# Attention preparation in a fused attention and feed-forward kernel: one lead for every pair of heads, loads listed by attention position, VectorE work in single pieces

## The chip, the cores and the metric

The kernel runs on one core of one Trainium2 chip. The metric is device time in microseconds (us) of one execution. The kernel before took 451.32 us in the median of 20 runs (449.64 to 452.49).

## What is computed

Attention with 8 batches, 8 heads, a sequence of 1152 and a head dimension of 64, whose queries are averaged in neighbouring twos (so 576 queries per head), is followed by a feed-forward block on 4608 tokens of width 512. Cut to what matters:

```python
q_pool = q.reshape(B, H, S // 2, 2, D).mean(axis=3)
scores = (1.0 / np.sqrt(D)) * np.matmul(q_pool, k.transpose(0, 1, 3, 2))
attn = np.exp(scores - scores.max(-1, keepdims=True)); attn = attn / attn.sum(-1, keepdims=True)
x = np.matmul(attn, v).transpose(0, 2, 1, 3).reshape(B * 576, 512)   # 4608 x 512
a = x @ w1                     # 4608 x 1024
b = x @ w2                     # 4608 x 1024
out = (a * b @ w3) @ w_out     # 4608 x 512
```

The kernel multiplies `w3` and `w_out` once (its T), so that the last line is one product per token tile.

## The kernel before

Two heads form a pair; there are 32 pairs, numbered P. The scores of all pairs, laid end to end, are cut into chunks of 512 columns per head. An iteration `it` of the main loop (162 of them) issues two chunks. A pair is 5184 such columns, or 5.06 iterations, and the attention position `at` is `it * 1024 / 5184`, in pairs.

One iteration emits, in this order, onto the engines:

- TensorE: the score matmuls of two chunks (`scores`, L187), which read `kT[P]` and `qT[P]`, the transposed keys and queries. ScalarE: one exponential per chunk (`expo`, L193) from the PSUM tile `psc` (two buffers) into the ring `er`.
- Preparation of later pairs, if it is due (see below).
- TensorE: the products of finished exponentials with `vt` (`attend`, L206) into the PSUM tile `po`, of which there is one buffer. When a pair is complete, `normalize` (L216, L218) has VectorE write `xn`, which frees `po`, and SyncE's queue transposes `xn` into `xT` by two DMAs.
- TensorE: filler. `fill(due)` pulls matmuls from generators until a count of modelled TensorE time, `busy`, reaches `due`, which grows by `PACE0` or `PACE1` in each iteration. The fillers are `gen_T` (transposes of `w3`, L250, and products with `w_out`, L265), from iterations `T_AT` on, and `gen_ffn` (L278, L291, L301), one unit per 512 tokens, from three iterations after the attention of its tokens is done. Filler and preparation share the two PSUM buffers of tag `ff`. What is left of the filler after the loop, and the last two units, run in a tail.

Each engine carries out its own instructions in the order in which they are emitted. The order is written by hand (`manual_schedule`); waits between engines come from the tiles and their buffer counts.

Preparation of pair P starts from three loads, `load(P)`: keys into `kst` (4 buffers, L90), queries into `qst` (3 buffers for two pairs each, L83), values into `vst` (4 buffers, L97). All loads, those of the weights too, go out from GpSimd's queue in the order of emission, and cast from 4-byte to 2-byte numbers. A DMA from this queue uses one of eight semaphores in turn, so it is issued only when the eighth DMA before it has landed; a load into a reused buffer also waits until VectorE has read the old contents.

- Pairs 0 to 7 (`NPE`): `prep_stage` emits three VectorE operations at once, the sum of neighbouring queries (`pool_q`, L119), a reordering copy of the keys into `kc` (L148) and the copy of the values into `vt` (L128), 0.8 pairs ahead. `prep_pe`, 0.5 pairs ahead, finishes the filler's open PSUM group (`fill(0, settle=True)`) and then emits 18 TensorE transposes (L158, L163) and three copies out of PSUM (L164, L168, L169), ahead of the iteration's `attend`. Those transposes are not added to `busy`. For pair 0 ScalarE makes the large copy (L166).
- Pairs from 8 on: `prep_dma` emits the three VectorE operations (L135, L119, L128) and two transposing DMAs on SyncE's queue (L136 into `kT`, L138 into `qT`) in one iteration. Its lead is 1.0 pair for pair 8, 1.5 for pair 9 and 1.6 from pair 10 on:

```python
lead = 0.5 if prepped < NPE else min(1.6, 0.5 + 0.5 * (prepped - NPE + 1))
```

For even P from 8 on, one `pool_q` sums the queries of P and P+1 together.

Of the kernel before, what the change touches and what calls it, by code (L numbers as in the profile page):

```python
# [8 lines left out]
FP16 = mybir.dt.float16  # L9
# [6 lines left out]
NJ = 9  # L16
# [7 lines left out]
def kernel(  # L24
# [11 lines left out]
    nc = tc.nc  # L36
    B, H, S, D = q.shape
# [5 lines left out]
    NP = B * H // 2  # L43
    SCL = 16.0
    NPE = 8
    T_AT = (8, 14)

    T_MM, T_TR, T_SC, T_AV = 0.216, 0.06, 0.63, 0.061
    PACE0, PACE1 = 2.2, 2.19
    SCALE = 0.5 * float(D) ** -0.5  # L50

# [2 lines left out]
    ab = ctx.enter_context(tc.tile_pool(name="ab", bufs=4))  # L54
    ffp = ctx.enter_context(tc.tile_pool(name="ffp", bufs=2))
    psum = ctx.enter_context(
        tc.tile_pool(name="psum", bufs=1, space=bass.MemoryType.PSUM))

    xT = const.tile([128, NC, NT], FP16)
    w1sb = const.tile([128, NC, dff], FP16)  # L60
    w2sb = const.tile([128, NC, dff], FP16)
# [6 lines left out]
    ident = const.tile([128, 128], FP16)  # L68
# [7 lines left out]
    kst, vst, qst, kT, qT, qps = {}, {}, {}, {}, {}, {}  # L76

    def load_q(P):
        if P % 2 == 0:
            qst[P // 2] = stage.tile([128, 2, 18, D], FP16, tag="qst", bufs=3, name="qst")  # L80
        b, h0 = P // 4, 2 * (P % 4)
        o = 64 * (P % 2)
        nc.gpsimd.dma_start(  # L83
            out=qst[P // 2][o:o + 64].rearrange("p u t d -> p u (t d)"),
            in_=q[b, h0:h0 + 2].rearrange("u (p t) d -> p u (t d)", t=18))

    def load_k(P):
        b, h0 = P // 4, 2 * (P % 4)
        kst[P] = stage.tile([128, 2, NJ, D], FP16, tag="kst", name="kst")
        nc.gpsimd.dma_start(  # L90
            out=kst[P].rearrange("p u j d -> p u (j d)"),
            in_=k[b, h0:h0 + 2].rearrange("u (p j) d -> p u (j d)", j=NJ))

    def load_v(P):
        b, h0 = P // 4, 2 * (P % 4)
        vst[P] = stage.tile([128, 2, NJ, D], FP16, tag="vst", name="vst")
        nc.gpsimd.dma_start(  # L97
            out=vst[P].rearrange("p u j d -> p u (j d)"),
            in_=v[b, h0:h0 + 2].rearrange("u (p j) d -> p u (j d)", j=NJ))

    def load(P):
        if P < NP:
            load_k(P)
            load_q(P)
            load_v(P)

    def pool_q(P):

        pp, o = P // 2, 64 * (P % 2)
        if P % 2 == 0:  # L110
            qps[pp] = ab.tile([128, NJ, 2, D], FP16, tag="qp", bufs=2, name="qp")
        if P < NPE:
            r = slice(o, o + 64)
        elif P % 2 == 0:
            r = slice(0, 128)
        else:
            return
        src = qst[pp][r].rearrange("p u (c two) d -> p u c two d", two=2)
        nc.vector.tensor_tensor(  # L119
            out=qps[pp][r].rearrange("p c u d -> p u c d"),  # L120
            in0=src[:, :, :, 0, :], in1=src[:, :, :, 1, :], op=ALU.add)

    def new_kq(P):
        kT[P] = ab.tile([128, NJ, 128], FP16, tag="kT", bufs=3, name="kT")
        qT[P] = ab.tile([128, NJ, 64], FP16, tag="qT", bufs=3, name="qT")

    def copy_v(P):
        nc.vector.tensor_copy(out=vts[P % 4][:, :, :, 0:D], in_=vst.pop(P))  # L128

    def prep_dma(P):  # L130

        pp, o = P // 2, 64 * (P % 2)
        new_kq(P)
        kc = ab.tile([128, NJ, 2, D], FP16, tag="kc", bufs=2, name="kc")
        nc.vector.tensor_copy(out=kc.rearrange("p j u d -> p u j d"), in_=kst.pop(P))  # L135
        nc.sync.dma_start_transpose(out=kT[P], in_=kc.rearrange("p j u d -> p (j u d)"))  # L136
        pool_q(P)
        nc.sync.dma_start_transpose(  # L138
            out=qT[P], in_=qps[pp][o:o + 64].rearrange("p c u d -> p (c u d)"))
        copy_v(P)  # L140

    kcs = {}

    def prep_stage(P):

        pool_q(P)
        kcs[P] = ab.tile([128, NJ, 2, D], FP16, tag="kc", bufs=2, name="kc")
        nc.vector.tensor_copy(out=kcs[P].rearrange("p j u d -> p u j d"), in_=kst.pop(P))  # L148
        copy_v(P)

    def prep_pe(P):
        pp, o = P // 2, 64 * (P % 2)
        new_kq(P)
        kc = kcs.pop(P)
        t2 = psum.tile([128, 1024], FP16, tag="ff", bufs=2, name="t2")
        t1 = psum.tile([128, 1024], FP16, tag="ff", bufs=2, name="t1")
        for c in range(NJ):
            nc.tensor.transpose(t2[:, 128 + 64 * c:192 + 64 * c],  # L158
                                qps[pp][o:o + 64, c].rearrange("p u d -> p (u d)"),
                                ident[o:o + 64, o:o + 64])  # L160
        for j in (8, 0, 1, 2, 3, 4, 5, 6, 7):
            dst = t1[:, 128 * j:128 * j + 128] if j < 8 else t2[:, 0:128]
            nc.tensor.transpose(dst, kc[:, j].rearrange("p u d -> p (u d)"), ident)  # L163
        nc.vector.tensor_copy(out=qT[P].rearrange("p c f -> p (c f)"), in_=t2[:, 128:704])  # L164
        if P == 0:
            nc.scalar.copy(out=kT[P][:, 0:8].rearrange("p j f -> p (j f)"), in_=t1)  # L166
        else:
            nc.vector.tensor_copy(out=kT[P][:, 0:8].rearrange("p j f -> p (j f)"), in_=t1)  # L168
        nc.vector.tensor_copy(out=kT[P][:, 8], in_=t2[:, 0:128])  # L169


    psc = {}
# [60 lines left out]
    def load_w3(i):  # L233
        t = ffp.tile([128, 4, dff], FP16, tag="g", name="w3h")
        nc.gpsimd.dma_start(
            out=t, in_=moe_w3.rearrange("(c p) f -> p c f", p=128)[:, 4 * i:4 * i + 4])
        w3h.append(t)

    def load_w(dst, src):
        nc.gpsimd.dma_start(out=dst, in_=src.rearrange("(c p) f -> p c f", p=128))  # L240
# [31 lines left out]
    def gen_ffn(t, tail):  # L272
# [25 lines left out]
        for i in range(4):  # L298
# [13 lines left out]
            for s in range(2):  # L312
# [13 lines left out]
        out=ident, in_=ident, compare_op=ALU.not_equal, fill=1.0,  # L326
        base=0, channel_multiplier=1, pattern=[[-1, 128]])
    load_v(0)
    load(1)
    load(2)  # L330
    load_w3(0)
    load_w(wosb, moe_w_out)
    load(3)
    load_w3(1)
    waiting = [lambda: load(4), lambda: load_w(w1sb, moe_w1), lambda: load_w(w2sb, moe_w2),
               lambda: load(5), lambda: load(6)]
    loaded, staged, prepped = 7, 1, 1
    prep_stage(0)
    prep_pe(0)

    n_units = NT // 512
    filler = []
    next_unit = 0
    busy = due = 0.0
# [4 lines left out]
    def fill(until, settle=False):  # L349

        nonlocal busy, whole
        while filler and (not whole if settle else busy < until):
            try:
                cost, whole = next(filler[0])
                busy += cost
            except StopIteration:
                filler.pop(0)

    for it in range(NIT):
        if it in T_AT:  # L360
            filler.append(gen_T(T_AT.index(it)))

        while next_unit < n_units:
            last_b = (512 * (next_unit + 1) - 1) // SQ
            if (last_b + 1) * 4 * PAIR + 3 * 2 * CH > it * 2 * CH:
                break
            filler.append(gen_ffn(next_unit, False))
            next_unit += 1
        scores(2 * it)
        expo(2 * it)  # L370
        scores(2 * it + 1)
        expo(2 * it + 1)
        busy += T_SC
        due = (due if filler else busy - T_SC) + (PACE0 if it < 20 else PACE1)
        at = it * 2 * CH / PAIR
        if staged < NPE and at >= staged - 0.8:
            prep_stage(staged)
            staged += 1
            if waiting:
                waiting.pop(0)()  # L380
                if waiting:
                    waiting.pop(0)()
            else:
                load(loaded)
                loaded += 1
        lead = 0.5 if prepped < NPE else min(1.6, 0.5 + 0.5 * (prepped - NPE + 1))
        if prepped < NP and at >= prepped - lead:
            if prepped < NPE:
                fill(0, settle=True)
                prep_pe(prepped)  # L390
            else:
                prep_dma(prepped)
                load(loaded)
                loaded += 1
            prepped += 1
        ready = [b for b in blocks[nb:nb + 40]
                 if b[0] * SQ + min(128 * b[1] + 128, SQ) <= 2 * it * CH]

        last = [n for n, (J, i) in enumerate(ready) if J % NJ == NJ - 1 and i == 4]
        if last:  # L400
            ready = ready[:last[0] + 1]
        busy += T_AV * len(ready)
        for J, i in ready:
            attend(J, i)
        if last:
            normalize(ready[-1][0] // NJ)
        nb += len(ready)
        fill(due)
    for J, i in blocks[nb:]:
        attend(J, i)  # L410
    normalize(NP - 1)
# [37 lines left out]
```

The softmax here doesn't subtract the row's maximum and nothing guards it: scores larger than these inputs give would overflow.

## Time and profile before

| | us |
|---|---|
| median of 20 runs | 451.32 |
| the profiled execution, its own time | 451.45 |
| its span, first to last instruction | 449.7 |
| TensorE matmuls busy | 419.6 |
| ScalarE busy | 329.9 |
| VectorE busy | 198.3 |

1.75 us of the profiled execution lie outside its span. Matmuls are pipelined and their ends are modelled, so a TensorE that shows busy is not TensorE at its peak; what counts is where it is idle. In a line of the timeline the columns are start, duration, engine, line, operation, tiles written and read, shape where it is kept, the number of instructions merged, and in brackets the engine's idle time before it with what ended it. In the table of waits the columns are the waiting line, what it waited for, the sum in us, the number of times and the longest. PE is TensorE's matmul row, PEld its weight loads, ACT ScalarE, DVE VectorE, POOL GpSimd, SPq the queue of SyncE.

### The profile page before, as it was taken

To read this page: it belongs to the slowest core of one execution; us is meant where nothing else is said; L and a number is where in the kernel's file an instruction comes from. 1 tells how busy PE (TensorE), PEld (TensorE's weight loads), DVE (VectorE), ACT (ScalarE), POOL (GpSimd) and SP (SyncE) were. 2 spreads that over 40 slices of the span, in tenths; PEclk is the share of its full clock that TensorE was granted. 3 is DMA by queue.
4 is the path that set the end of the run, shared out by engine and by line. 5 is a ranking of instruction groups with operands and counts; after the bars stand their busy time and mean duration, and the time that the engine had idled before them with its cause. 6 is when DMAs were issued, how large, how long until landed. Compare 5 with 4: busy or idle time off the path is not lost.

```text
span 449.7 us, 12036 instructions
## 1 busy us (share of the span) xinstructions
PE 419.6 (93%) x5168; PEld 223.1 (50%) x5168; DVE 198.3 (44%) x347; ACT 329.9 (73%) x350; POOL 69.7 (15%) x107
## 2 busy tenths in 40 slices
PE   1889899999599999999999999999999999989996
PEld 1555464554255555555555555545555555544442
DVE  2245453565145534554345444544455344433130
ACT  2877777778388888888878888888888888823332
POOL 7312131113011111111111111111100000000000
PEclk9999999999699999999999999999999999999999
DMA  8999999658999989998899999969892461121304
GB/s 129 209 182 207 210 188 190 97 89 121 118 200 156 146 145 166 172 138 131 137 189 134 128 147 203 134 112 171 163 153 64 88 103 25 15 67 41 88 7 93
DMA packets 94468, 59.11 MB, mean 131 GB/s; under 512 B 66256, under 2 KB 83664, under 8 KB 94416
## 3 DMA queue, kind: packets, MB, share of 16 engines
q0 software_dynamic: 25168, 33.56, 48.6%
q1 hardware_dynamic: 69248, 24.79, 35.5%
q8 instruction: 40, 0.66, 0.6%
q14 instruction: 12, 0.10, 0.1%
HBM read 67.11 MB, written 9.44 MB: 170 GB/s over the span
## 4 chain that ended last, share of the span: by engine, by line
PE 83%; DMA 5%; ACT 4%; DVE 4%; issue 3%; SPq 1%; POOL 0%; ACTq 0%; DVEq 0%; POOLq 0%
PE po L206 21%; PE psc L187 20%; PE pb L291 13%; PE pa L278 13%; PE pp L301 12%; ACT er L193 3%; PE pT L265 3%; DMA qT<-qp 3%; DMA kst<-in_k_dram 1%; PE t L163 1%; DVE xn L218 1%; DVE kT L168 1%; PE w3t L250 1%; DMA out_dram<-osb 1%; DVE T L269 0%
## 5 line engine op out<-in xcount | busy, mean ns | idle before, releaser
L193 ACT ACTIVATE er<-psc 128x1024 f16<-128x1024 f32 x324 | 313.5, 1022 | 72.1 <-PE psc L187 69.2
L187 PE MATMUL psc<-qT,kT 64*128 64x512 f16 (+7 forms) x1152 | 109.4, 291 | 11.3 <-DMA qT<-qp 5.5
L206 PE MATMUL po<-vt,er 128*128 128x65 f16 x2880 | 116.7, 194 | 0.3 <-DVE xn L218 0.2
L206 PEld LDWEIGHTS <-er 128*128 128x128 f16 x2880 | 97.5, 98 | 35.5 <-issue 32.0
L187 PEld LDWEIGHTS <-kT 64*128 64x128 f16 x1152 | 44.2, 95 | 95.8 <-issue 84.2
L291 PE MATMUL pb<-xT,w2sb 128*128 128x512 f16 x288 | 79.7, 379 | 2.4 <-DVE osb L310 1.3
L278 PE MATMUL pa<-xT,w1sb 128*128 128x512 f16 x288 | 79.1, 379 | 1.2 <-DVE asb L287 0.7
L296 DVE TENSOR_TENSOR gT<-pb,asb 128x512 f16<-128x512 f32 x72 | 49.6, 689 | 64.1 <-PE pb L291 63.6
L301 PE MATMUL pp<-T,gT 128*128 128x512 f16 x288 | 71.0, 382 | 0.0
L287 DVE COPY asb<-pa 128x512 f32<-128x512 f32 x56 | 38.6, 689 | 47.0 <-PE pa L278 47.0
L90 POOL DMA_DIRECT2D kst<-in_k_dram x32 | 22.9, 715 | 221.1 <-DVE kc L135 174.7
L310 DVE TENSOR_SCALAR osb<-pp 128x512 f32<-128x512 f32 x28 | 19.3, 690 | 53.4 <-PE pp L301 51.0
L301 PEld LDWEIGHTS <-gT 128*128 128x128 f16 x288 | 25.5, 98 | 24.4 <-issue 0.6
L278 PEld LDWEIGHTS <-w1sb 128*128 128x128 f16 x288 | 25.8, 97 | 23.8 <-issue 0.7
L291 PEld LDWEIGHTS <-w2sb 128*128 128x128 f16 x288 | 25.4, 97 | 23.6 <-issue 1.6
L285 ACT COPY asb<-pa 128x512 f32<-128x512 f32 x16 | 9.4, 586 | 24.5 <-PE pa L278 24.5
L218 DVE TENSOR_TENSOR xn<-po,rz 128x640 f16<-128x640 f32 x32 | 26.4, 825 | 1.3 <-DVE rz L216 0.2
L97 POOL DMA_DIRECT2D vst<-in_v_dram x32 | 23.2, 725 | 16.4 <-DMA w3h<-in_moe_w_dram 5.6
L216 DVE RECIPROCAL rz<-po 128x10 f32<-128x10 f32 x32 | 7.1, 221 | 38.1 <-PE po L206 38.0
L83 POOL DMA_DIRECT2D qst<-in_q_dram x32 | 19.6, 612 | 8.9 <-DMA w2sb<-in_moe_w_dram 4.2
L119 DVE TENSOR_TENSOR qp<-qst 128x1152 f16<-128x1152 f16 (+1 forms) x20 | 15.0, 751 | 6.4 <-DMA qst<-in_q_dram 6.3
L265 PE MATMUL pT<-wosb,w3T 128*128 128x512 f16 x64 | 16.5, 379 | 1.2 <-DVE w3T L252 1.2
(29 smaller groups left out, 96.5 us busy)
## 6 DMA issues: line engine op xcount, KB each, us to landing
qst<-in_q_dram POOLq DMA_DIRECT2D x32, 288.0 KB, 6.9
kst<-in_k_dram POOLq DMA_DIRECT2D x32, 288.0 KB, 5.3
vst<-in_v_dram POOLq DMA_DIRECT2D x32, 288.0 KB, 9.1
out_dram<-osb SPq DMA_DIRECT2D x72, 128.0 KB, 3.1
w3h<-in_moe_w_dram POOLq DMA_DIRECT2D x2, 1024.0 KB, 20.5
wosb<-in_moe_w_out_dram POOLq DMA_DIRECT2D x1, 1024.0 KB, 19.3
xT<-xn SPq DMA_TRANSPOSE x64, 3.5
w1sb<-in_moe_w_dram POOLq DMA_DIRECT2D x1, 1024.0 KB, 21.4
```

The lines of the kernel that those rows point to most:

```text
L90: nc.gpsimd.dma_start(out=kst[P].rearrange("p u j d -> p u (j d)"), in_=k[b, h0:h0 + 2].rearrange("u (p j) d -> p u (j d)", j=NJ))
L97: nc.gpsimd.dma_start(out=vst[P].rearrange("p u j d -> p u (j d)"), in_=v[b, h0:h0 + 2].rearrange("u (p j) d -> p u (j d)", j=NJ))
L187: nc.tensor.matmul(t[:, u, o:o + ln], kT[P][s, j, :], qv[s, f0:f0 + ln], start=True, stop=True)
L193: nc.scalar.activation(out=er[:, :, r:r + CH], in_=psc.pop(c), func=AF.Exp, bias=0.0, scale=SCALE)
L206: nc.tensor.matmul(po[P][:, u, VW * i:VW * i + D + 1], er[:, u, r:r + 128], vts[P % 4][:, u, j, 0:D + 1], start=(j == 0 and i == 0), stop= ...
L218: nc.vector.tensor_tensor(out=xn.rearrange("p i u d -> p u i d"), in0=acc[:, :, :, 0:D], in1=rz.to_broadcast([128, 2, 5, D]), op=ALU.mult)
L265: nc.tensor.matmul(pt, w3T[:, c, a, :], wosb[:, a, :], start=(a == 0), stop=(a == NF - 1))
L278: nc.tensor.matmul(pa, w1sb[:, mc, ft * 128:ft * 128 + 128], xT[:, mc, t0:t0 + 512], start=(mc == 0), stop=(mc == NC - 1))
L287: nc.vector.tensor_copy(out=asb, in_=pa)
L291: nc.tensor.matmul(pb, w2sb[:, mc, ft * 128:ft * 128 + 128], xT[:, mc, t0:t0 + 512], start=(mc == 0), stop=(mc == NC - 1))
L296: nc.vector.tensor_mul(out=gT[:, ft, :], in0=pb, in1=asb)
L301: nc.tensor.matmul(pp, gT[:, ft, 128 * i:128 * i + 128], T16[:, ft, :], start=(ft == 0), stop=(ft == NF - 1))
```

## The change

- `prep_dma` is split into `dma_k` and `dma_q`, `prep_stage` into `pool_q`, `copy_k` and `copy_v`. Each becomes an entry of a list `side`, and one entry is taken per iteration, after the filler, except in an iteration that completes a pair.
- The entries are made 1.8 pairs ahead for every pair from 8 on, pair 8 included, and 1.3 pairs ahead for pairs below 8.
- `pe_kq` (formerly `prep_pe`) is emitted after the iteration's `attend` instead of before it; the filler's open group is finished at the end of the iteration before; its 18 transposes are added to `busy`. Its first PSUM tile is filled before the second is taken. For pair 0 the large copy is shared between ScalarE and VectorE, and the values are copied after the transposes.
- At the start the loads of pair 2 come after the first half of `w3` and after `w_out` in the list, not before them. Further loads are listed at fixed positions `at`: pairs 3 and 4 at 0.4, `w1` and `w2` at 1.0, pair P at P - 3 from pair 5 on.
- `T_AT` becomes (7, 13), `T_TR` 0.042, and `PACE0` holds for 40 iterations instead of 20.

```diff
-    T_AT = (8, 14)
-    T_MM, T_TR, T_SC, T_AV = 0.216, 0.06, 0.63, 0.061
+    T_AT = (7, 13)
+    T_MM, T_TR, T_SC, T_AV = 0.216, 0.042, 0.63, 0.061
...
-    def prep_dma(P):
-
-        pp, o = P // 2, 64 * (P % 2)
-        new_kq(P)
-        kc = ab.tile([128, NJ, 2, D], FP16, tag="kc", bufs=2, name="kc")
-        nc.vector.tensor_copy(out=kc.rearrange("p j u d -> p u j d"), in_=kst.pop(P))
-        nc.sync.dma_start_transpose(out=kT[P], in_=kc.rearrange("p j u d -> p (j u d)"))
-        pool_q(P)
-        nc.sync.dma_start_transpose(
-            out=qT[P], in_=qps[pp][o:o + 64].rearrange("p c u d -> p (c u d)"))
-        copy_v(P)
...
-    def prep_stage(P):
-
-        pool_q(P)
+    def copy_k(P):
         kcs[P] = ab.tile([128, NJ, 2, D], FP16, tag="kc", bufs=2, name="kc")
         nc.vector.tensor_copy(out=kcs[P].rearrange("p j u d -> p u j d"), in_=kst.pop(P))
-        copy_v(P)
-
-    def prep_pe(P):
+
+    def dma_k(P):
+        new_kq(P)
+        copy_k(P)
+        nc.sync.dma_start_transpose(
+            out=kT[P], in_=kcs.pop(P).rearrange("p j u d -> p (j u d)"))
+
+    def dma_q(P):
+        pool_q(P)
+        o = 64 * (P % 2)
+        nc.sync.dma_start_transpose(
+            out=qT[P], in_=qps[P // 2][o:o + 64].rearrange("p c u d -> p (c u d)"))
+
+    def pe_kq(P):
...
         if P == 0:
-            nc.scalar.copy(out=kT[P][:, 0:8].rearrange("p j f -> p (j f)"), in_=t1)
+            nc.scalar.copy(out=kTP[:, 512:1024], in_=t1[:, 512:1024])
+            nc.vector.tensor_copy(out=kTP[:, 0:512], in_=t1[:, 0:512])
...
     load(1)
-    load(2)
     load_w3(0)
     load_w(wosb, moe_w_out)
-    load(3)
+    load(2)
     load_w3(1)
-    waiting = [lambda: load(4), lambda: load_w(w1sb, moe_w1), lambda: load_w(w2sb, moe_w2),
-               lambda: load(5), lambda: load(6)]
-    loaded, staged, prepped = 7, 1, 1
-    prep_stage(0)
-    prep_pe(0)
+
+    loads = [(0.4, lambda: load(3)), (0.4, lambda: load(4)),
+             (1.0, lambda: load_w(w1sb, moe_w1)), (1.0, lambda: load_w(w2sb, moe_w2)),
+             (2.0, lambda: load(5)), (3.0, lambda: load(6)), (4.0, lambda: load(7))]
+    loads += [(P - 3.0, lambda P=P: load(P)) for P in range(8, NP)]
...
+    pool_q(0)
+    copy_k(0)
+    pe_kq(0)
+    copy_v(0)
...
-        due = (due if filler else busy - T_SC) + (PACE0 if it < 20 else PACE1)
+        due = (due if filler else busy - T_SC) + (PACE0 if it < 40 else PACE1)
         at = it * 2 * CH / PAIR
-        if staged < NPE and at >= staged - 0.8:
-            prep_stage(staged)
+        while loads and at >= loads[0][0]:
+            loads.pop(0)[1]()
+        if staged < NP and at >= staged - (1.3 if staged < NPE else 1.8):
+            if staged < NPE:
+                side += [lambda P=staged: pool_q(P), lambda P=staged: copy_k(P)]
+            else:
+                side += [lambda P=staged: dma_k(P), lambda P=staged: dma_q(P)]
+            side.append(lambda P=staged: copy_v(P))
             staged += 1
...
-        lead = 0.5 if prepped < NPE else min(1.6, 0.5 + 0.5 * (prepped - NPE + 1))
-        if prepped < NP and at >= prepped - lead:
-            if prepped < NPE:
-                fill(0, settle=True)
-                prep_pe(prepped)
-            else:
-                prep_dma(prepped)
-                load(loaded)
-                loaded += 1
-            prepped += 1
...
         nb += len(ready)
+        if prep_now:
+            pe_kq(prepped)
+            busy += 18 * T_TR
+            prepped += 1
         fill(due)
+
+        if side and not last:
+            side.pop(0)()
+        prep_now = prepped < NPE and at >= prepped - 0.7 and prepped in kcs
+        if prep_now:
+            fill(0, settle=True)
```

## The prediction

> **What bounds the kernel now.** I read the page first: the engine shares, then the slices.
>
> ```profile
> PE 419.6 (93%) x5168; PEld 223.1 (50%) x5168; DVE 198.3 (44%) x347; ACT 329.9 (73%) x350; POOL 69.7 (15%) x107
> ...
> PE   1889899999599999999999999999999999989996
> ...
> PEclk9999999999699999999999999999999999999999
> DMA  8999999658999989998899999969892461121304
> ```
>
> TensorE is the bound almost everywhere. Its idle time is 449.7 - 419.6 = 30.1 us, so the change can gain only where TensorE waits. The slices (11.2 us each) show two places: the start, and slice 11, where the clock drops too. The timeline there:
>
> ```profile
> 109.74 1.94 ACT L193 ACTIVATE er<-psc 128x1024 f16<-128x1024 f32 x2 [0.34 <-PE psc L187]
> 109.79 0.72 PE L206 MATMUL po<-vt,er 128*128 128x65 f16 x18
> ...
> 112.01 1.02 ACT L193 ACTIVATE er<-psc 128x1024 f16<-128x1024 f32 x1 [0.33 <-PE psc L187]
> 112.90 7.50 SPq L138 DMA_TRANSPOSE qT<-qp  x1
> 117.38 0.61 PE L187 MATMUL psc<-qT,kT 64*128 64x512 f16 x2 [5.47 <-DMA qT<-qp]
> 117.92 1.17 PE L206 MATMUL po<-vt,er 128*128 128x65 f16 x18
> ...
> 121.44 1.94 ACT L193 ACTIVATE er<-psc 128x1024 f16<-128x1024 f32 x2 [2.33 <-PE psc L187]
> ```
>
> Pair 8 is the first with transposing DMAs and has the shortest lead. Its qT was issued at 104.54 and landed 12.70 later (the chain of waits has that piece, "104.54 12.70 DMA qT<-qp"); TensorE stood for 5.47 us. Afterwards 18 attention matmuls took 1.17 us instead of 0.72. Iterations begin at the exponentials: this one lasts 121.44 - 112.01 = 9.43 us, the one before 2.27.
>
> The start decides the rest. The timeline, and for four loads the answer for their tile in a window that holds only them, with the delay from issue to landing:
>
> ```profile
> L90 POOL DMA_DIRECT2D kst<-in_k_dram x1: 723/723/723, 6.0 to 6.0; - x1
> ...
> DMA to landing us min/median/max: 9.5/9.5/9.5
> ```
> ```profile
> L235 POOL DMA_DIRECT2D w3h<-in_moe_w_dram x1: 765/765/765, 8.4 to 8.4; - x1
> ...
> DMA to landing us min/median/max: 15.7/15.7/15.7
> ```
> ```profile
> L240 POOL DMA_DIRECT2D wosb<-in_moe_w_out_dram x1: 887/887/887, 9.8 to 9.8; - x1
> ...
> DMA to landing us min/median/max: 19.3/19.3/19.3
> ```
> ```profile
> 25.08 0.82 DVE L218 TENSOR_TENSOR xn<-po,rz 128x640 f16<-128x640 f32 x1
> ...
> 26.38 1.20 PE L206 MATMUL po<-vt,er 128*128 128x65 f16 x34
> ```
>
> Pair 2's keys land at 15.4, the first half of w3 at 24.1, w_out at 29.1; likewise pair 2's queries (issued 6.7, 10.2 later) at 16.9 and its values at 18.1. They land in the order of the list, each load of a pair some 1.45 us after the one before, w3 6.0 after v2, w_out 5.1 after w3. The last two lines show what hangs on VectorE here: xn at 25.08 frees po, and pair 1's first attention matmuls follow at 26.38.
>
> Last, the table of waits and the loop's end:
>
> ```profile
> POOL kst L90 <- DVE kc L135: 174.7, 19, 15.2
> ```
> ```profile
> 403.74 0.69 DVE L310 TENSOR_SCALAR osb<-pp 128x512 f32<-128x512 f32 x1 [2.39 <-DMA out_dram<-osb]
> 404.48 1.02 PE L291 MATMUL pb<-xT,w2sb 128*128 128x512 f16 x4 [1.28 <-DVE osb L310]
> ```
>
> GpSimd's queue runs far ahead and stands for 174.7 us at the key buffer: buffers, not the place in the listing, set when loads start. At 404.48 TensorE waits 1.28 us because an output buffer was not yet stored.
>
> **What the Trainium skill says.** "DMA: Bandwidth & Descriptors", section on queues, rings and completion order: an engine takes descriptors of one ring in order and goes round robin between queue rows. The landings above agree for GpSimd's queue. "TensorE: Matmul & The Clock Gate", Part 1: after about one idle window of 3.4 us the array runs at half clock until a busy window has passed; here the clock fell after 5.47 us of idling. The same Part says that VectorE's queue is strictly first in, first out, so an operation that waits for a load holds up all behind it. I use that below; no wait of this kind long enough to test it stands in the trace.
>
> **The change, part by part**, against the profiled execution's 451.45 us (449.7 span and 1.75 outside).
>
> 1. *Pair 8's lead.* Counted in the code, its qT goes out at the end of iteration 34 instead of in 36, and is first read in the middle of 40: some 5.4 iterations of 2.28 us = 12.3 us of cover, where the DMA took 12.7. That one shared the engines with six loads and pair 9's transposes; now pair 9's are issued three iterations later and half the loads lie in between. Steady rows with a full set of loads took 11.1 (qT at 138.9) and less. So it lands in time, and the whole excess goes: 9.43 - 2.27 = 7.2 us. At worst only the idling goes, 5.5; should it still be late by some us, less. I take -7.2. What is late next there: nothing; TensorE goes on with filler.
>
> 2. *Pair 2's loads behind w3 and w_out.* The first six loads end at 13.8 (v1) as before. Then w3 to 13.8 + 6.0 = 19.8, w_out to 24.9, k2 26.4, q2 27.8. But `pool_q(2)` is now emitted in iteration 4 (about 20 us), where before it came in iteration 7. Behind it on VectorE are `copy_k(2)` and normalize(0), which frees po. Then: 27.8 + 0.75 (pool_q) + 0.46 (copy) + 0.22 + 0.82 (normalize) + gaps 0.15 = 30.2. TensorE needs po at 26.4 and has nothing else in its queue: 3.8 us of idling, and ScalarE soon stands too. Part comes back: iteration 7 does 16 w3 transposes and 8 products now, so I compare at iteration 9. After: 30.2 + 34 attention matmuls 1.4 + transposes 1.05 + wait 0.3 + 8 x 0.216 + scores 0.3 = 34.9, plus iteration 8 (scores, 18 attention matmuls, 18 transposes) 2.25 = 37.1. Before: 32.55, with 5 products fewer (1.08). Loss 37.1 - 32.55 - 1.08 = 3.5. With q2 from 26.8 (w3 as quick as w_out) to 30.5 (the 1.8 us extra that k3 took after w_out, and more) it is 2.5 to 6.2. Idling of 3.8 us may or may not cool the clock: 0 to 2 us (4 us at half clock at most, as after pair 8), I take 1. Sum +4.5, range +2.5 to +8.
>
> 3. *Ramp, iterations 9 to 39.* Before: 112.01 - 32.55 = 79.5 us. Its content: 31 bases of 1.20 (scores and 18 attention matmuls), 134 products x 0.216 = 28.9, 48 w3 transposes 3.7, five sets of 18 transposes 5.25, together 75.1; so 4.4 are waits (copies before the filler's bank comes free, ScalarE after overlong iterations). `pe_kq`, now counted in `busy`, leaves its iteration no filler, and the three copies out of PSUM, 0.46 + 0.69 + 0.22 = 1.37, lie beside the next scores and attention (1.2 to 1.3). Iteration 24 has no filler and idles 0.6. I leave 2.0: -2.4, range 0 to -3.
>
> 4. *Single pieces, iterations 41 to 161.* TensorE idles 268.0 - 266.05 = 1.95 us from 122 to 390, mostly where normalize, kc, qp and vt (2 to 3 us on VectorE) met an evacuation. I take -0.8; a piece in a new bad place could cost 1. The split puts qT one iteration after kT; both still have over 15 us.
>
> 5. *Loop's end.* Eight filler matmuls fewer run in the loop (699, not 707), so after the last attention 37 remain instead of 29; the last four outputs come after xn's transposes have left SyncE's queue, and the third output buffer is stored in time. -1.3, or 0.
>
> 6. *Start.* In the listing VectorE's half of pair 0's copy waits for ScalarE's half: 0.59 + about 0.4 against 1.01 before: 0, within 0.2. PACE, T_TR and T_AT move filler, not its amount: 0. Listing loads by position moves nothing, since POOL waits for buffers and earlier landings alone.
>
> Sum: -7.2 + 4.5 - 2.4 - 0.8 - 1.3 = -7.2. 451.45 - 7.2 = 444.25; the median stands 0.13 below the profiled run, so 444.2.
>
> **The rivals.**
> - *No block at pair 2*: if q2 landed by 23 us, point 2 vanishes: 451.3 - 11.7 = 439.6. For it: nothing but a faster w3; against: the landings in order. 0.10.
> - *The block eats the gain*: q2 at 30.5, cooled clock, and points 3 to 5 bring nothing: -7.2 + 8 = +0.8, 452. For it: pair 3's queries follow the second half of w3 (about 38 to 39 us) and `pool_q(3)` asks at about 39. 0.11, spread over 449.5 to 452.5.
> - *Slower: even pairs block VectorE.* `pool_q(P)`, P even, needs the queries of P + 1 too, listed at P - 2, only two iterations before. If loads did follow the listing, each would land 7.6 us (0.7 + the median 6.9) after its start, 3 us late; less 1.2 of cover, 1.8 x 12 pairs = 22: 451.3 - 7.2 + 22 = 466. It decides from 0.6 us per pair. Against: the 174.7 us above, and loads wait only for buffers freed about 5 pairs ahead. 0.07.
> - *Pair 8 still late* by 2 to 4 us, the change not doing what it says: 446 to 448. 0.08.
>
> **How the numbers follow.** The forecast has 0.64, its own range 441 to 448. Below 440 lies most of the first rival, above 449.5 the second and third; so 440 to 449.5 leaves out two in ten. About 0.2% (0.9 us) is what a measurement of this kernel can tell from no change. Faster: 0.64 + 0.10 + 0.08 + 0.03 of the second = 0.85; same 0.05; slower 0.10.
>
> **What would show it.** Pair 8: no wait of TensorE for qT, no clock drop at slice 11, and iteration 40 near 2.3 us. Pair 2: VectorE idle before qp for q2 until about 28, TensorE idle 3 to 5 us before pair 1's attention at about 30, perhaps half clock after it. The end: no wait for osb. The forecast is wrong if q2 lands by 23, if VectorE waits for loads at later even pairs, or if iterations 9 to 39 keep their 4.4 us of waits.

## The result, and the profile after

The changed kernel takes 446.27 us in the median of 7 runs (445.47 to 446.95), the kernel before 450.89 in the median of 48 (448.39 to 452.49): a ratio of 0.9895, with a 95% interval of 0.9877 to 0.9913. The forecast was 444.2, in a range of 440.0 to 449.5. A ratio leaves out runs more than 1.5% over the fastest of their kernel; for e1 below these would be half of all, so there I give medians alone. The profiled execution took 445.19 us (span 443.3), the one of before 451.45 (449.7).

From the page after, first the engines, then the slices that answer to those of before:

```profile
PE 419.4 (95%) x5168; PEld 223.7 (50%) x5168; DVE 197.5 (45%) x348; ACT 329.5 (74%) x350; POOL 69.9 (16%) x107
...
PE   2869899999999999999999999999999999999995
...
PEclk9989999999999999999999999999999999999999
```

TensorE is busy as long as before (419.4 against 419.6); its idle time fell from 30.1 to 443.3 - 419.4 = 23.9 us. The hole in slice 11 is gone, in the row of the clock too. A new, smaller hole stands in slice 2, with an 8 under it in the clock's row. The forecast named both places. Pair 8's in the timeline, and the answer for its qT in a window that holds only its issue:

```profile
112.19 0.60 PE L188 MATMUL psc<-qT,kT 64*128 64x512 f16 x4
...
112.68 1.94 ACT L194 ACTIVATE er<-psc 128x1024 f16<-128x1024 f32 x2 [0.33 <-PE psc L188]
112.73 0.72 PE L207 MATMUL po<-vt,er 128*128 128x65 f16 x18
...
114.95 1.94 ACT L194 ACTIVATE er<-psc 128x1024 f16<-128x1024 f32 x2 [0.33 <-PE psc L188]
```
```profile
L145 SPq DMA_TRANSPOSE qT<-qp x1: 1207/1207/1207, 102.2 to 102.2; - x1
...
DMA to landing us min/median/max: 5.2/5.2/5.2
```

Iteration 40 lasts 114.95 - 112.68 = 2.27 us, where it lasted 9.43. The four score matmuls at 112.19 are the last two of pair 7 and, from 112.42, the first two of pair 8, and they wait for nothing. But mark the last line: the transpose took 5.2 us from issue to landing. It had taken 12.7, and I had expected about 11. That is more than an earlier start explains, and the experiments go after it.

The start, in the timeline after:

```profile
26.87 0.75 DVE L119 TENSOR_TENSOR qp<-qst 64x1152 f16<-64x1152 f16 x1 [6.28 <-DMA qst<-in_q_dram]
...
28.16 0.82 DVE L219 TENSOR_TENSOR xn<-po,rz 128x640 f16<-128x640 f32 x1
...
29.04 2.06 PE L207 MATMUL po<-vt,er 128*128 128x65 f16 x34 [2.89 <-DVE xn L219]
```

This is the block at pair 2, one line below the other: VectorE waits 6.28 us for pair 2's queries; normalize, emitted behind them, starts at 28.16 although po had been complete for a while; TensorE waits 2.89 us for po. The 34 attention matmuls then take 2.06 us instead of the 1.20 of before, and the granted clock reads 0.50 from 28.9 to 32.3. The Trainium skill ("TensorE: Matmul & The Clock Gate", Part 1) says that VectorE's queue is strictly first in, first out; the forecast had no wait long enough to test that, and now the 6.28 us one agrees.

The loop's end and GpSimd's wait for key buffers:

```profile
397.31 0.69 DVE L311 TENSOR_SCALAR osb<-pp 128x512 f32<-128x512 f32 x1 [1.03 <-PE pp L302]
398.05 1.02 PE L292 MATMUL pb<-xT,w2sb 128*128 128x512 f16 x4
```
```profile
POOL kst L90 <- DVE kc L134: 116.9, 21, 8.6
```

The wait for the stored output buffer is gone. GpSimd stood for 174.7 us at the key buffers; it still stands for 116.9 there, and for 78.2 at the value buffers, so most loads go out when a buffer comes free, as before.

The two traces cut at the same iterations, with 0.216 us for each filler product that one of them has more:

| stretch | before, us | after, us | products | difference, predicted | measured |
|---|---|---|---|---|---|
| start to iteration 9 | 32.55 | 37.22 | 5 more | +4.5 | 4.67 - 1.08 = +3.6 |
| 9 to 39 | 79.46 | 75.46 | 13 fewer | -2.4 | -4.0 + 2.8 = -1.2 |
| iteration 40 | 9.43 | 2.27 | 1 more | -7.2 | -7.16 - 0.22 = -7.4 |
| 41 to 161 | 273.03 | 272.94 | 1 fewer | -0.8 | +0.1 |
| 161 to the end | 55.23 | 55.41 | 8 more | -1.3 | 0.18 - 1.73 = -1.55 |
| sum | | | | -7.2 | -6.4 |

The spans differ by 6.4, the profiled executions by 6.26, the medians by 4.6. The profiled run after lies 1.1 us under its median, that of before 0.56 over its own. I come back to the 1.1.

### The profile page after: what moved, and what is told of

It is laid out like the page before. It is cut to its first block, busy times and chain, and to the rows that moved or that the text cites. A ratio compares the mean times of both kernels' runs of the same rounds, so it can differ in the third digit from the quotient of the medians.

```text
span 443.3 us, 12036 instructions
## 1 busy us (share of the span) xinstructions
PE 419.4 (95%) x5168; PEld 223.7 (50%) x5168; DVE 197.5 (45%) x348; ACT 329.5 (74%) x350; POOL 69.9 (16%) x107
## 4 chain that ended last, share of the span: by engine, by line
PE 88%; DMA 4%; DVE 2%; issue 2%; POOL 2%; ACT 2%; ACTq 0%; POOLq 0%
PE po L207 22%; PE psc L188 20%; PE pb L292 14%; PE pa L279 13%; PE pp L302 13%; DMA qst<-in_q_dram 4%; PE pT L266 3%; ACT er L194 1%; PE w3t L251 1%; PE t L155 0%; POOL kst L90 0%; PE t L161 0%; DVE xn L219 0%; DVE T L270 0%; DVE kT L169 0%
## 5 line engine op out<-in xcount | busy, mean ns | idle before, releaser
L302 PE MATMUL pp<-T,gT 128*128 128x512 f16 x288 | 69.9, 379 | 0.0
L90 POOL DMA_DIRECT2D kst<-in_k_dram x32 | 22.9, 716 | 147.8 <-DVE kc L134 116.9
L97 POOL DMA_DIRECT2D vst<-in_v_dram x32 | 23.0, 719 | 88.1 <-DVE vt L128 78.2
L119 DVE TENSOR_TENSOR qp<-qst 128x1152 f16<-128x1152 f16 (+1 forms) x20 | 15.0, 750 | 12.3 <-DMA qst<-in_q_dram 12.2
```

What stands on the lines that cost most here:

```text
L90: nc.gpsimd.dma_start(out=kst[P].rearrange("p u j d -> p u (j d)"), in_=k[b, h0:h0 + 2].rearrange("u (p j) d -> p u (j d)", j=NJ))
L97: nc.gpsimd.dma_start(out=vst[P].rearrange("p u j d -> p u (j d)"), in_=v[b, h0:h0 + 2].rearrange("u (p j) d -> p u (j d)", j=NJ))
L302: nc.tensor.matmul(pp, gT[:, ft, 128 * i:128 * i + 128], T16[:, ft, :], start=(ft == 0), stop=(ft == NF - 1))
```

## The experiments

My theory at this point: (a) pair 8's stall went because of the longer lead; (b) the pair-2 block costs some 3.5 to 4.5 us and comes from the loads' new place in GpSimd's queue together with the new place of the query sum in VectorE's; (c) the single pieces do little. The rivals: for (a), the stall went because the pieces are spread over iterations, or because fewer loads run beside the transposes; for (b), the idling of slice 2 has another cause, such as the weights. Each expectation below stood before its run.

Each variant ran beside the kernel before on one chip, and the medians of the kernel before differ: 450.03 beside e1 to e4, 450.41 beside e5 to e8, 450.55 beside e9 to e11, 450.30 beside e12, 450.89 beside the changed kernel. So up to 0.9 us of a difference between the medians of two kernels from different groups need not come from the kernels. The changed kernel gains 4.6 us over the kernel before beside it; "own gain" below is the same for a variant.

**One part alone, on the kernel before.** e1: pair 8 gets the full lead, nothing else changes.

```diff
-        lead = 0.5 if prepped < NPE else min(1.6, 0.5 + 0.5 * (prepped - NPE + 1))
+        lead = 0.5 if prepped < NPE else 1.6
```

> The kernel before, with pair 8 alone prepared as early as the later pairs (it falls in iteration 34 instead of 36). My theory, that pair 8's late qT is worth 7.2 us and independent of the rest: 450.9 - 7.2 = 443.7, no TensorE wait for qT, no clock drop near 115 us. Rival, that only the 5.5 us of idling comes back or that the stall moves to pair 9: 445.5 or above.

Measured: a median of 450.18 over 22 runs, against 450.03 for the kernel before on the same chip, and a wide spread, 443.58 to 453.03. The traced run happened to be the fastest, 443.58, and had no stall: qT took 10.4 us, and the time from its issue to the moment when TensorE asked for it, its cover, was 11.2. So the lead alone can bring the 7 us, and mostly doesn't. (a) is in doubt.

e9 is the same kernel once more, for a trace of an ordinary run.

> The kernel with pair 8 alone prepared earlier, once more, for a trace of an ordinary execution: most of its executions took 448 to 451, the one traced took 443.6, with pair 8's qT landing 10.4 us after its issue and 11.3 us of cover. If the cover is too short at times: qT(8) or kT(8) lands over 11.3 us after the issue and TensorE waits for it, some us with a half clock after it, 446 to 451. If the stall has moved to pair 9 or to the start, the wait stands there. If nothing is late: 443 to 445 again, and it stays open.

Measured: 453.06 us, in one run. Its timeline and the answer for the same transpose:

```profile
118.28 0.61 PE L187 MATMUL psc<-qT,kT 64*128 64x512 f16 x2 [6.04 <-DMA qT<-qp]
...
118.82 1.17 PE L206 MATMUL po<-vt,er 128*128 128x65 f16 x18
```
```profile
L138 SPq DMA_TRANSPOSE qT<-qp x1: 1681/1681/1681, 100.9 to 100.9; - x1
...
DMA to landing us min/median/max: 17.3/17.3/17.3
```

Issued 3.7 us earlier than before, qT lands 17.3 us later, and TensorE, which asked after 11.4 us, waits longer (6.04) than it did with the ramp (5.47). The tables by stretch show what the DMA engines did, first e9, then the traced e1 (columns at the end: clock; time of the DMA packets as a share of the engines' time, which can pass 1; GB/s):

```profile
104.00:110.00 6.00, 6.00 (x82) 3.10 (x79) 3.51 (x7) 5.14 (x6) 2.04 (x3) 1.00 1.56 71
```
```profile
103.00:109.00 6.00, 6.00 (x82) 3.10 (x79) 3.50 (x7) 5.13 (x6) 2.04 (x3) 1.00 1.55 200
```

The same instructions, the same 6 us of the program, the same busy share: 71 GB/s in one and 200 in the other. A busy share tells nothing of progress here.

e2: on the kernel before, only the loads of pair 2 move behind w3 and w_out.

```diff
-    load(2)
     load_w3(0)
     load_w(wosb, moe_w_out)
+    load(2)
```

> The kernel before, with the loads of pair 2 listed behind the first half of w3 and w_out and nothing else. My theory, that late loads cost only because their VectorE operations now stand ahead of normalize(0): here normalize(0) is emitted first, so VectorE waits about 1 us for q2 with nobody behind it; 450.9 + 0 to 0.5. Rival, that the late landing itself costs: pair 1's attention stays on time but pair 2 is late, 450.9 + 3 or more.

Measured: ratio 1.0034 [1.0017, 1.0052], 22 runs, 451.3 against 450.03. q2 landed at 27.2, but pair 2's query sum is emitted behind normalize(0) there, and iteration 9 begins at 32.61 (before 32.55). Late loads alone cost little: 1.3 us in the median, more than the 0 to 0.5 expected, and the trace does not show where. Pair 8's stall stood much as before (4.91 us).

e8: on the kernel before, pair 9's preparation moves away from pair 8's, to iteration 40; pair 8 keeps its lead of 1.0.

```diff
-        lead = 0.5 if prepped < NPE else min(1.6, 0.5 + 0.5 * (prepped - NPE + 1))
+        lead = 0.5 if prepped < NPE else {8: 1.0, 9: 1.2}.get(prepped, 1.6)
```

> The kernel before, pair 8 as late as it was (iteration 36), but pair 9 prepared in iteration 40 instead of 38, so that its transposes and the loads that it sets free do not fall into the landing of pair 8's qT. If the short lead alone makes the stall: 450.9 within 1. If the collision with pair 9 makes it: qT lands within about 8 us, the wait shrinks to below 1.5 us, 444 to 446. My prediction said lead and mentioned the collision; in the changed kernel qT took only 5.2 us, which speaks for the collision.

Measured: 447.79, ratio 0.9949 [0.9927, 0.9971], 10 runs. qT took 9.6 us and the stall was 2.33. That lies between the two forecasts: pair 9's preparation is part of the crowd, not all of it.

e12: on the kernel before, the lead stays, and the preparation of every pair from 8 on is cut into three pieces (keys, queries, values with the next loads) that go out in successive iterations.

```diff
-                prep_dma(prepped)
-                load(loaded)
-                loaded += 1
+                pend += [lambda P=prepped: dma_k(P), lambda P=prepped: dma_q(P),
+                         lambda P=prepped: end_v(P)]
             prepped += 1
+        if pend:
+            pend.pop(0)()
```

> The kernel before with its ramp, but with the three pieces of a pair from 8 on in three iterations, one each, the loads that they set free behind the last. So pair 8's kT goes out in iteration 36 as before and its qT one iteration later, with only some 6 us of cover. What the runs so far suggest: pieces in one iteration gave 9.6 to 17.3 us from issue to landing of pair 8's qT in seven traces, pieces spread 5.2 to 5.7 in six, so qT lands near its first use and TensorE waits at most 1.5 us: 444 to 446. If the lead is what matters after all, the shorter cover makes it worse: TensorE waits 4 us or more, 450 or above.

Measured: 447.47, ratio 0.9931 [0.9909, 0.9954], 16 runs. qT went out at 106.99, 2.4 us later than before, and landed in 6.6 us instead of 12.7; a stall of 2.15 us stayed, more than the 1.5 expected, since the cover was now 4.6 us and too short. This run also sets pair 8's loads apart, and pair 9's pieces.

**One part undone, on the changed kernel.** e10 takes pairs 8 and 9 back to leads of 1.0 and 1.5, with all three pieces in one iteration.

```diff
-        if staged < NP and at >= staged - (1.3 if staged < NPE else 1.8):
+        if staged in (8, 9) and at >= staged - (1.0 if staged == 8 else 1.5):
+            dma_k(staged)
+            dma_q(staged)
+            copy_v(staged)
+            staged += 1
+        elif staged < NP and staged not in (8, 9) and at >= staged - (1.3 if staged < NPE else 1.8):
```

> The changed kernel, with pairs 8 and 9 prepared as before: all three pieces in iterations 36 and 38. My theory, that the ramp is the whole of the 7.2 us: qT of pair 8 takes 12 us again, a TensorE wait of 5 us, clock drop, 446.3 + 7 = 453. Rival, that the changed loads leave the DMA engines freer there and the wait shrinks to 2 us: 449.

Measured: 452.27, ratio 1.005 [1.0029, 1.0071], 8 runs: slower than before. qT took 12.4 us, the stall was 5.17 and cooled the clock. Without what the change does for pairs 8 and 9, the rest of it loses: that part is worth 452.27 - 446.27 = 6.0 us in medians, 6.3 by own gains (-1.7 against 4.6). The changed order of the loads alone does not take the stall away.

e6 keeps the early lead, but emits the pieces of a pair from 8 on in one iteration.

```diff
-        if side and not last:
+        while side and not last:
             side.pop(0)()
+            if staged <= NPE:
+                break
```

> The changed kernel, with the three VectorE pieces of a pair emitted in one iteration again, for pairs from 8 on. My prediction gave the single pieces 0.8 us, so 447.1. What the trace of the changed kernel suggests, that iterations 41 to 161 take as long as before: 446.3 within 0.4.

Measured: 446.38, ratio 0.9916 [0.9897, 0.9935], 5 runs, within the noise the time of the changed kernel; its own gain is 4.0, 0.6 less. qT took 10.1 us, but had been issued at 98.6 with 14.2 us of cover, so nothing waited. At pair 8 a lead that is long enough does without the spreading. Later on it does not quite: one qT comes too late, and iterations 41 to 161 last 273.86 us against 272.94.

```profile
192.96 0.20 PE L188 MATMUL psc<-qT,kT 64*128 64x64 f16 x2 [0.75 <-DMA qT<-qp]
```

For pair 8, all traces side by side; the cover is the time from issue until TensorE asked for qT:

| kernel | pieces | qT issued | cover, us | to landing, us | stall, us |
|---|---|---|---|---|---|
| before | together | 104.5 | 7.4 | 12.7 | 5.47 |
| e1, e9 (lead) | together | 99.9, 100.9 | 11.2, 11.4 | 10.4, 17.3 | 0, 6.04 |
| e2 (order) | together | 104.6 | 7.4 | 12.1 | 4.91 |
| e10 (ramp back) | together | 105.7 | 7.4 | 12.4 | 5.17 |
| e6 (at once) | together | 98.6 | 14.2 | 10.1 | 0 |
| e8 (pair 9 later) | together | 103.4 | 7.4 | 9.6 | 2.33 |
| e12 (split alone) | spread | 107.0 | 4.6 | 6.6 | 2.15 |
| after | spread | 102.2 | 10.2 | 5.2 | 0 |
| e3, e4, e5, e7, e11 (all based on after) | spread | | 10.2 | 5.2 to 5.7 | 0 |

TensorE waits where the landing is longer than the cover, by about the difference. For pair 8 the landing takes 9.6 to 17.3 us together and 5.2 to 6.6 spread, with no overlap. For later pairs the effect is smaller and the two overlap: for the qT issued between 109.5 and 320 us it is 3.3 to 10.6 with a median of 7.1 in the changed kernel, and 5.0 to 12.3 with a median of 8.6 in e6. So a stall can be avoided by a short landing under a middling cover (after) or by a long cover (e6). Spreading alone leaves a stall (e12), and a lead of 11.2 us together mostly does too (e1).

e7: on the changed kernel, the loads are listed one pair earlier.

```diff
-    loads += [(P - 3.0, lambda P=P: load(P)) for P in range(8, NP)]
+    loads += [(P - 4.0, lambda P=P: load(P)) for P in range(8, NP)]
```

> The changed kernel, with the loads from pair 8 on listed 4 pairs ahead instead of 3. My theory, that buffers and earlier landings set when a load starts and not its place in the listing: no change within 0.4 us, and the issue times of the loads agree with those of the changed kernel within 1 us. Rival, that the listing paces the loads: they start about 11 us earlier, collide with other transposes, and the time moves by over 1 us.

Measured: 445.91, ratio 0.9903 [0.9884, 0.9922], 4 runs, as the changed kernel. The key loads go out within 0.15 us of the same times, but for five early ones (0.16 to 1.1 us). The positions in the listing set nothing from pair 8 on; the buffers do.

**The block at pair 2.** e3: on the changed kernel, pair 2's loads go back ahead of w3 and w_out.

```diff
+    load(2)
     load_w3(0)
     load_w(wosb, moe_w_out)
-    load(2)
```

> The changed kernel, with the loads of pair 2 listed ahead of w3 and w_out again. My theory: q2 lands near 17, VectorE does not wait, TensorE's 2.9 us of idling before pair 1's attention and the half clock after it go; 446.3 - 3.6 - about 1 = 442, at least 3 us below the changed kernel. Rival, that w3 and w_out then come too late for the filler that now starts in iteration 7 (they landed at 24 and 29 in the kernel before): the wait moves to the filler, 445 to 446.

Measured: 442.74, ratio 0.9837 [0.9806, 0.9869], 5 runs, 3.5 us under the changed kernel (own gain 7.3, so 2.7 more). q2 landed at 16.8, xn waited for nothing, and iteration 9 began at 34.33 instead of 37.22.

e4 leaves the loads late and mends the other half: pair 2's query sum is emitted behind normalize(0), the copy of its keys one iteration later.

```diff
-        if staged < NP and at >= staged - (1.3 if staged < NPE else 1.8):
+        if staged < NP and at >= staged - (1.0 if staged == 2 else 1.3 if staged < NPE else 1.8):
...
-        if side and not last:
+        if side and (not last or it == 6):
```

> The changed kernel, load order kept, with pair 2's query sum emitted in iteration 6 behind normalize(0) instead of in iteration 4, and its key copy in 7 instead of 5. My theory, that VectorE's order is the cause: xn near 25.5 us, TensorE goes on, 442 to 443. Rival, that TensorE needs pair 2's data as soon anyway: a wait at pair 2's transposes in iteration 8, 445 to 446.

Measured: 442.2, ratio 0.9837 [0.9796, 0.9879], 6 runs, 4.1 us under the changed kernel (own gain 7.8, so 3.2 more). Its timeline:

```profile
24.10 0.82 DVE L219 TENSOR_TENSOR xn<-po,rz 128x640 f16<-128x640 f32 x1
...
25.41 1.20 PE L207 MATMUL po<-vt,er 128*128 128x65 f16 x34
...
27.07 0.75 DVE L119 TENSOR_TENSOR qp<-qst 64x1152 f16<-64x1152 f16 x1 [2.14 <-DMA qst<-in_q_dram]
```

The queries land at 27.0, as late as in the changed kernel, and VectorE still waits for them, 2.14 us. But xn now stands in front: it starts at 24.10, and the 34 attention matmuls follow at 25.41, at full clock. So neither the late load nor the early sum does much harm alone: e2 has the first without the second, e3 the second without the first, and e4 again the first without the second, in the changed kernel.

e5: on the changed kernel, an iteration that holds the 18 transposes of `pe_kq` issues no filler after them.

```diff
-        fill(due)
+        else:
+            fill(due)
```

> The changed kernel, with no filler in an iteration that holds the 18 transposes. In the changed kernel's trace one product follows the transposes in iterations 13 and 18 and waits 0.78 us each for the copies out of PSUM. My theory: those two waits go, about 1.5 us, 444.7. Rival, that TensorE then meets the same copies one step later: no change within 0.3 us.

Measured: 444.01, ratio 0.9867 [0.9844, 0.9891], 4 runs, 2.3 us under the changed kernel (own gain 6.4, so 1.8 more). The line that it answers, in the changed kernel's timeline:

```profile
48.22 0.69 DVE L169 COPY kT<-t 128x1024 f16<-128x1024 f16 x1
...
48.97 0.38 PE L266 MATMUL pT<-wosb,w3T 128*128 128x512 f16 x1 [0.78 <-DVE kT L169]
```

One product right behind the transposes needs the PSUM bank that they filled and waits until VectorE has copied it out. That happened twice (iterations 13 and 18), 0.78 us each, with the next scores queued behind it on TensorE. In e5 both waits are gone; its iterations 9 to 39 last 73.71 us against 75.46.

e11 has the edits of e4 and e5 together.

> The changed kernel, with both mends: pair 2's query sum behind normalize(0), and no filler in an iteration with the 18 transposes. Against the kernel before, the first mend alone gave 442.2 and the second alone 444.0, both from 446.3. If they add: 442.2 - 1.6 = 440.6. If the first has already moved the second's waits under other ones: 442.

Measured: 440.47 (439.42 to 441.07), ratio 0.9783 [0.9756, 0.981], 5 runs, the best version: 5.8 us under the changed kernel, about e4's 4.1 and e5's 2.3 added (6.4); by own gains 5.5, against 3.2 and 1.8 added (5.0). The main waits of TensorE that are left in its loop, from its table of waits:

```profile
PE psc L188 <- ACT er L194: 3.8, 9, 0.7
PE pT L266 <- DVE T L270: 1.8, 2, 1.5
...
PE pT L266 <- DVE w3T L253: 0.8, 1, 0.8
```

The wait for xn and those of pT for kT are no longer in it. Of the 1.8, 1.46 is one wait, which e4 has too (1.50): pair 3's queries, which land at 38.0 (38.4 in e4), hold up the copy of T on VectorE, the pair-2 block in small.

## Why the prediction was right, and where its reasons were not

The forecast lay 2.1 us under the median, inside its range. 0.9 of it is in the profiled execution (444.25 forecast, 445.19 measured), 1.1 is what this execution lies under its median. In the parts, errors of both signs cancel in good measure.

1. *Pair 8's lead: size right by luck, reason half wrong.* Predicted -7.2, measured -7.16 in length. The step said that the lead gives 12.3 us of cover and that a landing of 11.1 or less fits under it. Both figures were off. qT was issued at 102.18 and first read at 112.42: the cover was 10.2 us, 4.5 iterations and not 5.4. A landing of 11.1 would have left TensorE waiting for some 0.9 us. What saved the step is that the landing fell to 5.2, and that comes from spreading the pieces, which it did not count: in e6, which undoes the spreading alone, the landing takes 10.1. The lead does the rest: spread pieces with 4.6 us of cover (e12) gain only 2.8, and with the pieces together 11.2 us of cover (e1) gain nothing in the median, while 14.2 (e6) are enough. The step mentioned "half the loads lie in between" as a reason, and took the lead as the cause. With e1 as the change I would have forecast -7 and been wrong. Spreading moves apart the transposes and also the loads that they set free. Which of the two shortens the landing, and why e9 fell to 71 GB/s, was not found; that stays open.

2. *Pair 2's block: right.* q2 landed at 26.85 (27.8 forecast), TensorE waited 2.89 us (3.8), iteration 9 began at 37.22 (37.1), the loss was 3.6 with the cooled clock in it (3.5 and 1). 0.6 of it is luck: the first exponential came that much earlier (point 6), so the block itself cost 4.2. w3 landed at 18.5 and w_out at 24.0, each 1 us earlier than I had them. In medians the block is worth 3.5 (e3) to 4.1 (e4), by own gains 2.7 to 3.2. The 1.1 us that the profiled run lies under its median belongs here in good part: in other traces with the same start iteration 7 lasts 9.8 to 11.3 us, not 9.5, and the half clock 6.8 us, not 3.4, in three of them. The clock's row of e7:

```profile
PEclk9969999999999999999999999999999999999999
```

3. *Ramp, iterations 9 to 39: mis-sized.* -1.2, not -2.4. I had left 2.0 of the 4.4 us of waits and overlooked that a filler product can still follow the transposes in the same iteration; the two waits of 0.78 (1.6 us) are that. e5 takes them away and gains 1.75 us in this stretch.

4. *Single pieces, iterations 41 to 161: wrong by 0.9 against the kernel before.* Predicted -0.8, measured +0.1. TensorE's idle time there, 1.78 us from 122 to 388 against 1.95 from 122 to 390, hardly moved. On the changed kernel they are worth 0.9 there (e6), 0.75 of it in the one wait for qT. The step looked for meetings on VectorE; what the pieces changed was the landing of the transposes, at pair 8 most of all.

5. *Loop's end: right*, -1.55 (-1.3), and the wait for the output buffer went as forecast.

6. *Start: right*, 0. The first exponential came at 10.88, not 11.51, because the first keys landed at 7.16, not 8.07, which varies from 6.6 to 8.3 over these traces; from the last transpose to the first scores took 1.10 us before and 1.14 after.

The rivals fell: q2 didn't land by 23, later even pairs didn't block VectorE, pair 8 was not late, and the block cost half of the gain rather than all.

## What to carry to other kernels

A prefetch is judged by its landing time as much as by its lead: spread its steps over iterations, then see how much lead is needed, because steps issued together can take much longer to land (at pair 8 10.1 us against 5.2). On an engine that works in order, an operation that waits for a load belongs behind the work that another engine is waiting for; here a later place for pair 2's two VectorE operations gave 3 to 4 us with the load as late as ever. And look at what is emitted directly behind a new step: one filler matmul behind the transposes cost 0.8 us each time.

## What was not expected of the hardware

The clock also fell without a long wait. In e3 TensorE never idled over 0.52 us at once around 25 us, but it was busy for only 2.06 of 3.40 us, because ScalarE was the bound; the clock then read 0.50 for the next 3.40 us. Its table by stretch (the clock is the third column from the end):

```profile
23.20:26.60 3.40, 2.06 (x33) 1.16 (x30) 1.05 (x2) 3.40 (x4) 0.71 (x1) 1.00 1.24 208
26.60:30.00 3.40, 3.40 (x46) 3.06 (x43) 0.86 (x2) 1.12 (x2) 0.76 (x1) 0.50 1.15 211
```

The Trainium skill ("TensorE: Matmul & The Clock Gate", Part 1) ties the half clock to an idle window of about 3.4 us. The 3.4 us agrees: the slow phases within the loop lasted 3.4 or 6.8 us. "Idle" doesn't: here the clock fell after a stretch in which TensorE was busy for 60%. This share doesn't decide alone, either. The same thin stretch stands in the kernel before (22.65 to 26.06, busy for 2.07 of 3.41 us) and in e4 (21.70 to 25.11, 2.07 of 3.41), and the clock stayed full there. What decides was not found. Nor does a long wait have to end first: in the kernel before the clock fell at 114.54, 2.6 us into the wait of 5.47 us.

The DMA engines showed a busy share of 1.55 and 1.56 in two runs of one kernel and moved 200 GB/s in one, 71 in the other. The transpose of pair 8's qT, 64 x 1152, landed in 5.2 to 6.6 us with its pieces spread and in 9.6 to 17.3 us with them together, 10.4 and 17.3 in two runs of the same instructions.
